# Start addresses of the operand areas in a one-core FNet and SwiGLU kernel, and w_down operands half a block later

## The chip, the cores and the metric

The kernel runs on one NeuronCore of a Trainium2 chip. The metric is device time in microseconds of one execution, inputs and outputs in HBM. TensorE (PE, with its weight loads PEld), VectorE (DVE), ScalarE (ACT), GpSimd (POOL) and SyncE (SP, which here only issues DMAs) run their own instruction streams in order and wait for each other by semaphores.

## The reference, cut to what matters

```python
# x [2048, 640]; w_gate, w_up [640, 1536]; w_down [1536, 640]
xn = layernorm(x)
a, b = xn @ dft_hid_re.T, xn @ dft_hid_im.T
s = dft_seq_re @ a - dft_seq_im @ b
g = silu((silu(xn @ w_gate) * (xn @ w_up)) @ w_down)
out = x + s * g
```

All of it is float32.

## The kernel before

Every float32 operand of a product is split into two float32r parts: the high part is written by ScalarE (line 196, a copy with rounding), the low part, what rounding lost, by VectorE (line 201, or 203 where a scale goes in). A product is then three matmuls (`mm3`, lines 217 to 219): high by high, high by low, low by high. In `nc.tensor.matmul(o, w, m)` `w` is the stationary operand, 128 columns wide, loaded into the array ahead of the matmul (PEld, LDWEIGHTS), and `m` the moving one, 512 columns of four bytes.

The work goes through stages, which one after the other keep TensorE fed: four rounds of the DFT along the sequence (`seq`, one level of Strassen's algorithm each), then twice (j = 0 and 1, half the rows each) the DFT along the hidden axis (`hid`), the gate and up products (`gate_up`) and the product with w_down (`down`). `gate_up` runs over twelve blocks f of 128 columns of w_gate and w_up. A block has the seven Strassen products p1, p5, p6, p2, p3, p7, p4, of 6, 6, 6, 9, 9, 9 and 9 matmuls: 54 for a block, 648 for twelve. Each product goes to one PSUM bank. The last one, p4, is carried into the next block, behind that block's p5.

Memory is laid out by hand. Two big tiles are areas for buffers: `hl` for split operands and `raw` for float32 data and results. A third piece of memory is handed over once: until the end of the DFT rounds it is `raw2` (float32 sums), from then on `hl2`. `gate_weights` splits the weights of a block into four buffers: the one with the operands of p1 and p5 lies in `hl`, the three others in `hl2`, so that 42 of a block's 54 matmuls load stationary operands from `hl2`. Everything else that TensorE reads in the main stages, all moving operands among it, lies in `hl`. The profile writes `ps<-hl,hl` where the stationary operand is from `hl2`, `ps<-hl` where both are from `hl`, and the order of instructions writes `hl` with a number (`hl_2545`, `hl_2549`) for `hl2`, and `raw` with a number for `raw2`.

In the built program `hl` begins at byte 16,512 of a partition (16 x 1024 + 128), `raw` at 102,528, and `raw2`/`hl2` at 200,672 (195 x 1024 + 992, which is 32 past a multiple of 64). Buffers in the operand areas have sizes that are multiples of 512 bytes, so that their places within the area are too.

The order of instructions is planned. Each step is given a planned time: products one after the other (`step`, a fixed time for each matmul), what produces operands some lead ahead (`prod`), evictions behind (`post`). The steps are then sorted by that time, and each engine and each DMA queue gets its instructions in that order. `place` and `fit` choose an offset in its area for each buffer, so that two buffers that live at once don't overlap; they prefer a pause between the last use of the one and the first write of the next, and take a smaller or a negative one where room is short. With a negative one a write waits for the earlier buffer's reader.

`down_operands` makes the stationary operands of `down` once, while the gate blocks of j = 0 run: twenty pieces (`Tp`), each with up to one VectorE sum, a split (ScalarE, then VectorE) and two stores to DRAM from POOL (line 535), from where `down` fetches them. `gate_up` takes one piece in the middle of a block and one at its end: `next(spare, None)`.

Of the kernel before, what the change touches and what calls it, by code (L numbers as in the profile page):

```python
# [7 lines left out]
F32 = mybir.dt.float32  # L8
BF16 = mybir.dt.bfloat16
F32R = mybir.dt.float32r  # L10
# [3 lines left out]
P = 128  # L14
S, D, F = 2048, 640, 1536
TC = 512
# [4 lines left out]
CG = 4  # L21
EPS = 1e-5
MM = 0.226
HL_KB, RAW_KB, TURN_KB = 84, 94, 28


class Plan:
# [111 lines left out]
def tile_fnet_swiglu(  # L139
# [17 lines left out]
    one = ctx.enter_context(tc.tile_pool(name="one", bufs=1))  # L157
    dram = ctx.enter_context(tc.tile_pool(name="dram", bufs=1, space=bass.MemoryType.DRAM))
    psum = ctx.enter_context(tc.tile_pool(name="psum", bufs=1, space=bass.MemoryType.PSUM))
    ctx.enter_context(tc.manual_schedule())  # L160

    pl = Plan()
    hl_arena = one.tile([P, HL_KB * 256], F32R, name="hl")
    raw_arena = one.tile([P, RAW_KB * 256], F32, name="raw")
    space = {"hl": hl_arena, "raw": raw_arena}
    ps = psum.tile([P, 8, TC], F32, name="ps")
    mv = one.tile([P, NS, 2], F32, name="mv")
    sm = one.tile([P, 6, NS], F32, name="sm")
    bst = one.tile([P, 2, 2, 6], F32, name="bst")
    z = one.tile([P, TC], BF16, name="z")  # L170
    rowst = one.tile([P, 2, 2 * NS], F32, name="rowst")
    mr_dram = dram.tile([2 * S], F32, name="mr_dram")
    where = {}

    def raw(name, a=0, n=None):
        o = where[name]
        arena, size = pl.size[name]
        return space[arena][:, o + a:o + (size if n is None else a + n)]

    def hl(name, i, a=0, n=None):  # L180

        key = name, "hl"[i]
        o = where[key]
        arena, size = pl.size[key]
        return space[arena][:, o + a:o + (size if n is None else a + n)]


    def split(lead, dst, n, src, reads, a=0, scale=None, sub=0, low_lead=None):


        def like(ap):
            s = src()
            return ap.rearrange("p (a b) -> p a b", b=s.shape[2]) if len(s.shape) == 3 else ap

        def high():
            nc.scalar.activation(like(hl(dst, 0, a, n)), src(), AF.Copy, scale=1.0 if scale is None else scale)  # L196

        def low():
            hi, lo = like(hl(dst, 0, a, n)).bitcast(F32), like(hl(dst, 1, a, n))
            if scale is None:  # L200
                nc.vector.tensor_tensor(lo, src(), hi, op=ALU.subtract)  # L201
            else:
                nc.vector.scalar_tensor_tensor(lo, src(), scale, hi, op0=ALU.mult, op1=ALU.subtract)  # L203

        pl.prod(lead, high, reads, [(dst, "h", sub)])
        pl.prod(lead - 2 if low_lead is None else low_lead, low, [*reads, (dst, "h", sub)], [(dst, "l", sub)])

    def both(dst, *subs):
        return [(dst, p, s) for s in (subs or (0,)) for p in "hl"]
# [27 lines left out]
    def wide(ap):  # L237
        return ap.rearrange("p (a b) -> p a b", b=TC)
# [4 lines left out]
    def evict(dst, b, a=0, n=None, after=0.0):  # L243
        n = len(b) * TC if n is None else n
        pl.post(lambda: nc.scalar.activation(wide(raw(dst, a, n)), pair(b), AF.Copy),  # L245
                pkeys(b), [(dst, a)], after)
# [163 lines left out]
    def load_x(k, lead, eng):  # L410
        pl.prod(lead, lambda: eng.dma_start(raw(xn, k * D, D), x[k * P:(k + 1) * P, :]), [], [(xn, k)])
# [144 lines left out]
    def seq(k):  # L556
        j, ri = k // 2, k % 2
# [4 lines left out]
        fresh, shared = k == 0, k == 1  # L562
# [6 lines left out]
        def source(q, g):  # L569
            c, h = j + 2 * (q // 10 - 1), q % 10 - 1  # L570
            return cs[c, ri, 2 * h + g // 2, :, 2 * (g % 2):2 * (g % 2) + 2]

        def load(q, g, lead):
            seq.n += 1
            name = pl.buf(("c", seq.n), "raw", 2 * TC)
            pl.prod(lead, lambda: nc.sync.dma_start(wide(raw(name)), source(q, g)), [], [(name, 0), (name, 1)])
            return name

# [8 lines left out]
        def operand(p, g, name):  # L587
            s = pl.buf(("S", k, p, g), "hl", 4 * TC)
            high, low = LEAD.get((p, g), LEAD.get(p, LEAD["S"])) if fresh else LEAD["S"]
            split(high, s, 2 * TC, lambda: raw(name), [(name, 0), (name, 1)], low_lead=low)  # L590
            return s
# [152 lines left out]
        def p2(g):  # L744
            if fresh:
                for kk in (8 + 2 * g, 9 + 2 * g):
                    load_x(kk, 40 + 2 * g, nc.sync)
                layer_norm(8 + 2 * g, 2, *LEAD["xn", 4 + g], nc.gpsimd)
            return operand("p2", g, load(12, g, 11 if fresh else 20))

        def p6(g):
            if shared:
# [175 lines left out]
    def gate_up(j):  # L928
        X = xn_t(j)
        for half in range(2):  # L930
            for c in (1, 2):
                pl.buf(("h", j, half, c), "raw", 6 * TC)
        tail = []
        for f in range(NF):
            w = gate_weights(j, f)
            b2, b1, b3 = (7, 5, 6) if f % 2 == 0 else (2, 3, 4)
            wkeys = [both(w[0], 0, 256), both(w[1], 0, 384), both(w[2], 0, 384), both(w[3])]

            def wt(p, i, a=0, w=w):
                part, at = COL[p]  # L940
                return hl(w[part], i, at + a, P)

            first = {}

            def go(p, bank, direct=None, wt=wt, wkeys=wkeys, first=first):
                def is_first():
                    v = first.setdefault(bank, True)
                    first[bank] = False
                    return v

                todo = []
                for k in range(2):
                    todo.append((bank, lambda i, k=k: wt(p, i, k * P),
                                 lambda i, k=k: hl(X[p], i, k * TC, TC), is_first()))
                reads = wkeys[COL[p][0]] + both(X[p])
                if direct:
                    col, half = direct
                    todo.append((bank, lambda i: wt(col, i), lambda i: hl(X[half], i), False))
                    reads += both(X[half]) + wkeys[COL[col][0]]
                product(todo, reads)  # L960

            tmp = lambda what, f=f: pl.buf((what, j, f), "raw", TC)
            hname = lambda c, f=f: ("h", j, f // 6, c)
            at = f % 6 * TC
            go("p1", b2)
            s1 = tmp("s1")
            evict(s1, (b2,))
            go("p5", b3)
            n5 = tmp("n5")
            evict(n5, (b3,))  # L970
            if tail:
                tail.pop()()
            go("p6", b2)
            u2 = tmp("u2")
            evict(u2, (b2,))
            go("p2", b1, ("d1", "d1"))
            g1 = tmp("g1")
            combine(g1, (b1,), s1, ALU.add)
            pl.post(lambda g1=g1: nc.scalar.activation(raw(g1), raw(g1), AF.Silu, scale=-1.0), [(g1, 0)], [(g1, 0)])
            if j == 0:  # L980
                next(spare, None)
            u1, u = tmp("u1"), tmp("uu")

            def top_half():
                go("p3", b3, ("d2", "d1"))
                combine(u1, (b3,), u2, ALU.subtract)
                pl.post(lambda u1=u1, g1=g1, o=hname(1), at=at: nc.vector.tensor_tensor(
                    raw(o, at, TC), raw(g1), raw(u1), op=ALU.mult), [(g1, 0), (u1, 0)], [(hname(1), at)])

            def bottom_half():  # L990
                go("p7", b2, ("d2", "d2"))
                combine(u, (b2,), n5, ALU.subtract)

            for part in (top_half, bottom_half) if f < NF - 1 else (bottom_half, top_half):
                part()

            def last(go=go, b2=b2, u=u, o=hname(2), at=at, tmp=tmp):
                go("p4", b2, ("d4", "d2"))
                g2 = tmp("g2")
                pl.post(lambda: nc.scalar.activation(raw(g2), ps[:, b2, :], AF.Silu), [("ps", b2)], [(g2, 0)])  # L1000
                pl.post(lambda: nc.vector.tensor_tensor(raw(o, at, TC), raw(g2), raw(u), op=ALU.mult),  # L1001
                        [(g2, 0), (u, 0)], [(o, at)])

            tail.append(last)
            if j == 0:
                next(spare, None)
        tail.pop()()
# [66 lines left out]
    for j in range(2):  # L1074
        hid(j)
        gate_up(j)
        down(j)

    where.update(pl.place({"hl": HL_KB * 256, "raw": RAW_KB * 256, "raw2": TURN_KB * 256, "hl2": TURN_KB * 256}))
    uses = [{pl.size[n if n in pl.size else (n, "h")][0] for n in names if n in pl.size or (n, "h") in pl.size} | {  # L1080
        pl.size[n][0] for n in names if n in pl.size} for _, _, _, names, _ in pl.ops]
    turn = 1 + max(i for i, u in enumerate(uses) if "raw2" in u)
# [58 lines left out]
```

## Time and profile before

| | |
|---|---|
| time, median of 3 runs | 994.96 us (994.18 to 995.2) |
| time of the profiled execution | 993.83 us |
| its span (first to last instruction) | 991.9 us |
| PE busy, matmuls | 984.0 us (99%), 4300 |
| DVE / ACT / POOL busy | 71% / 49% / 11% of the span |
| granted TensorE clock | 1.00 |
| DMA | 184.54 MB, 186 GB/s on average |

The profiled execution's time is 1.9 us more than its span, and 1.13 us under the median of the three runs. A busy PE is not a PE at its peak, since matmuls overlap in the records: what counts is how far apart the starts of two matmuls are.

### The profile page before, as it was taken

Reading aid. Unit: us, or ns where it says so; the run is one execution under the profiler, and the core shown is the slowest. Engines: PE = TensorE matmul, PEld = TensorE weight load, DVE = VectorE, ACT = ScalarE, POOL = GpSimd, SP = SyncE. Lnnn points to the kernel's source line nnn. Section 1 sums busy time; section 2 is a strip of 40 time slices with the busy share of each in tenths; the row PEclk is TensorE's granted clock in tenths of the full one; section 3 lists DMA queues with packets and bytes.
Section 4 is the critical chain, followed back from the end, with each engine's and each line's share of the span. In section 5 each row is a group of like instructions: output and inputs, shape, how many; then the busy total and the mean of one; then the engine's idle time right before and its main releaser. Section 6 shows DMA issues by size and latency. Waiting matters only on the chain.

```text
span 991.9 us, 11749 instructions
## 1 busy us (share of the span) xinstructions
PE 984.0 (99%) x4300; PEld 803.7 (81%) x4300; DVE 699.8 (71%) x936; ACT 483.3 (49%) x706; POOL 105.9 (11%) x173
## 2 busy tenths in 40 slices
PE   9999999999999999999999999999999999999998
PEld 5888888888888888888788888888888888888886
DVE  6899769656865685566678786587586666665675
ACT  5786456444645463334655555343345444444342
POOL 0450220011001100010211110000010000000000
PEclk9999999999999999999999999999999999999999
DMA  9995887574758477752447246679950211124675
GB/s 339 286 218 165 251 241 232 179 193 123 205 162 222 128 221 225 235 187 81 171 163 268 101 171 203 204 230 372 323 191 23 85 54 54 53 90 155 212 247 183
DMA packets 73977, 184.54 MB, mean 186 GB/s; under 512 B 6720, under 2 KB 23360, under 8 KB 73920
## 3 DMA queue, kind: packets, MB, share of 16 engines
q1 hardware_dynamic: 59808, 131.35, 39.9%
q0 software_dynamic: 14112, 52.45, 19.0%
q8 instruction: 33, 0.54, 0.2%
q14 instruction: 24, 0.20, 0.1%
HBM read 149.42 MB, written 34.36 MB: 185 GB/s over the span
## 4 chain that ended last, share of the span: by engine, by line
PE 98%; ACT 1%; issue 1%; DVE 0%; POOL 0%; POOLq 0%
PE ps L217 32%; PE ps L218 32%; PE ps L219 32%; PE ps L228 1%; PE ps L460 1%; ACT raw L245 0%; ACT hl L196 0%; ACT L1088 0%; DVE raw L250 0%; POOL y_dram L839 0%; DVE hl L203 0%; DVE hl L201 0%; DVE raw L1059 0%; DVE raw L1061 0%; DVE raw L914 0%
## 5 line engine op out<-in xcount | busy, mean ns | idle before, releaser
L196 ACT ACTIVATE hl<-raw 128x1024 fp32r<-128x1024 f32 (+7 forms) x499 | 360.4, 765 | 284.7 <-PE ps L219 74.8
L201 DVE TENSOR_TENSOR hl<-raw,hl 128x1024 fp32r<-128x1024 f32 (+5 forms) x428 | 375.7, 907 | 136.3 <-ACT hl L196 72.1
L217 PE MATMUL ps<-hl 128*128 128x512 f32 x1088 | 422.8, 389 | 0.0
L218 PE MATMUL ps<-hl 128*128 128x512 f32 x1088 | 422.5, 388 | 0.0
L219 PE MATMUL ps<-hl 128*128 128x512 f32 x1088 | 422.0, 388 | 0.0
L217 PEld LDWEIGHTS ps<-hl 128*128 128x128 f32 x1088 | 204.3, 188 | 43.0 <-ACT hl L196 0.4
L218 PEld LDWEIGHTS ps<-hl 128*128 128x128 f32 x1088 | 204.3, 188 | 42.6 <-DVE hl L201 0.3
L219 PEld LDWEIGHTS ps<-hl 128*128 128x128 f32 x1088 | 204.3, 188 | 42.3 <-DVE hl L203 0.2
L245 ACT ACTIVATE raw<-ps 128x512 f32<-128x512 f32 (+1 forms) x120 | 78.3, 670 | 119.9 <-PE ps L219 117.4
L217 PE MATMUL ps<-hl,hl 128*128 128x512 f32 x336 | 133.3, 397 | 1.1 <-ACT raw L245 1.1
L218 PE MATMUL ps<-hl,hl 128*128 128x512 f32 x336 | 133.1, 396 | 0.0
L219 PE MATMUL ps<-hl,hl 128*128 128x512 f32 x336 | 133.1, 396 | 0.0
L250 DVE TENSOR_TENSOR raw<-ps,raw 128x512 f32<-128x512 f32 (+1 forms) x93 | 74.7, 804 | 62.9 <-PE ps L219 61.6
L217 PEld LDWEIGHTS ps<-hl,hl 128*128 128x128 f32 x336 | 63.3, 188 | 16.9 <-ACT raw L245 1.5
L219 PEld LDWEIGHTS ps<-hl,hl 128*128 128x128 f32 x336 | 63.3, 188 | 15.5
L218 PEld LDWEIGHTS ps<-hl,hl 128*128 128x128 f32 x336 | 63.2, 188 | 15.2
L1001 DVE TENSOR_TENSOR raw<-raw 128x512 f32<-128x512 f32 x24 | 16.6, 692 | 50.9 <-ACT raw L1000 50.9
L203 DVE SCALAR_TENSOR_TENSOR hl<-raw,hl 128x384 fp32r<-128x384 f32 (+4 forms) x71 | 41.2, 580 | 10.2 <-ACT hl L196 4.6
L914 DVE TENSOR_TENSOR raw<-raw 128x256 f32<-128x256 f32 (+1 forms) x96 | 47.8, 519 | 0.0
L581 POOL DMA_DIRECT2D raw<-in_cs x36 | 32.1, 964 | 124.2 <-DVE raw L584 65.4
L1063 POOL DMA_DIRECT2D out<-raw x10 | 6.7, 673 | 306.9 <-DVE raw L1061 215.7
L658 POOL DMA_DIRECT2D p_dram<-raw x24 | 17.4, 766 | 204.3 <-DVE raw L250 164.9
(55 smaller groups left out, 305.9 us busy)
## 6 DMA issues: line engine op xcount, KB each, us to landing
raw<-in_cs SPq DMA_DIRECT2D x82, 512.0 KB, 6.9
hl<-d_p SPq DMA_DIRECT2D x56, 384.0 KB, 4.0
raw<-in_cs POOLq DMA_DIRECT2D x36, 512.0 KB, 9.5
raw<-in_wb SPq DMA_DIRECT2D x24, 640.0 KB, 3.9
d_p<-hl POOLq DMA_DIRECT2D x28, 384.0 KB, 3.4
raw<-p_dram SPq DMA_DIRECT2D x8, 1280.0 KB, 9.8
p_dram<-raw POOLq DMA_DIRECT2D x16, 512.0 KB, 6.3
raw<-in_hd SPq DMA_DIRECT2D x20, 320.0 KB, 9.2
```

The lines of the kernel that those rows point to most:

```text
L196: nc.scalar.activation(like(hl(dst, 0, a, n)), src(), AF.Copy, scale=1.0 if scale is None else scale)
L201: nc.vector.tensor_tensor(lo, src(), hi, op=ALU.subtract)
L203: nc.vector.scalar_tensor_tensor(lo, src(), scale, hi, op0=ALU.mult, op1=ALU.subtract)
L217: nc.tensor.matmul(o, w(0), m(0), start=first, stop=False, skip_group_check=True)
L218: nc.tensor.matmul(o, w(0), m(1), start=False, stop=False, skip_group_check=True)
L219: nc.tensor.matmul(o, w(1), m(0), start=False, stop=True, skip_group_check=True)
L245: pl.post(lambda: nc.scalar.activation(wide(raw(dst, a, n)), pair(b), AF.Copy), pkeys(b), [(dst, a)], after)
L250: pl.post(lambda: nc.vector.tensor_tensor(wide(raw(dst, a, n)), pair(b), wide(raw(other)), op=op), [*pkeys(b), (other, 0)], [(dst, a)], after)
L581: pl.prod(lead, lambda: nc.gpsimd.dma_start(wide(raw(name)), source(q, g), accum_op=ALU.add), [], [(name, 0), (name, 1)], 8)
L658: pl.post(lambda: nc.gpsimd.dma_start(p_dram[ri, c, e0:e0 + len(b)].rearrange("k p t -> p k t"), wide(raw(name))), [(name, 0)], [("pd", ri ...
L914: pl.prod(lead, lambda o=o, a=a, b=b, op=op: nc.vector.tensor_tensor(o(), a(), b(), op=op), [(w, 0)], [(c, lead)])
L1001: pl.post(lambda: nc.vector.tensor_tensor(raw(o, at, TC), raw(g2), raw(u), op=ALU.mult), [(g2, 0), (u, 0)], [(o, at)])
```

## The change

The big tiles are allocated in another order. The small tiles come first, with a filler of 32 bytes, then `hl`; `raw` goes to a pool at the other end of the memory; the piece that is handed over (`raw2`, later `hl2`) then begins right behind `hl`. In the built program `hl` begins at 18,432 (18 x 1024), `raw2`/`hl2` at 103,424 (101 x 1024) and `raw` at 132,096. `hl` is 1 KB smaller (83 KB) and `raw` 992 bytes larger, so that all offsets are placed anew. Two of the loads of the first DFT round (p2, g = 1 and 2) go to `raw2` in place of `raw`. The first of the calls for w_down operands in `gate_up` is left out, so that each of the twenty pieces is made half a block later.

```diff
-HL_KB, RAW_KB, TURN_KB = 84, 94, 28
+HL_KB, RAW_KB, TURN_KB = 83, 95, 28
...
-    hl_arena = one.tile([P, HL_KB * 256], F32R, name="hl")
-    raw_arena = one.tile([P, RAW_KB * 256], F32, name="raw")
-    space = {"hl": hl_arena, "raw": raw_arena}
-    ps = psum.tile([P, 8, TC], F32, name="ps")
     mv = one.tile([P, NS, 2], F32, name="mv")
...
     rowst = one.tile([P, 2, 2 * NS], F32, name="rowst")
+    one.tile([P, 8], F32, name="pad")
+    right = ctx.enter_context(tc.tile_pool(name="right", bufs=1, side="right"))
+    space = {"hl": one.tile([P, HL_KB * 256], F32R, name="hl"), "raw": right.tile([P, RAW_KB * 256 - 8], F32, name="raw")}
+    ps = psum.tile([P, 8, TC], F32, name="ps")
...
-        def load(q, g, lead):
+        def load(q, g, lead, arena="raw"):
             seq.n += 1
-            name = pl.buf(("c", seq.n), "raw", 2 * TC)
+            name = pl.buf(("c", seq.n), arena, 2 * TC)
...
-            return operand("p2", g, load(12, g, 11 if fresh else 20))
+            return operand("p2", g, load(12, g, 11 if fresh else 20, "raw2" if fresh and g in (1, 2) else "raw"))
...
-            if j == 0:
+            if j == 0 and f:
                 next(spare, None)
...
-    where.update(pl.place({"hl": HL_KB * 256, "raw": RAW_KB * 256, "raw2": TURN_KB * 256, "hl2": TURN_KB * 256}))
+    where.update(pl.place({"hl": HL_KB * 256, "raw": RAW_KB * 256 - 8, "raw2": TURN_KB * 256, "hl2": TURN_KB * 256}))
```

On ScalarE, at the end of the first gate block of j = 0, this stood before (768 columns: a piece of w_down; `hl_2545`: gate weights; `raw<-ps`: evictions):

```order
L979 ACTIVATE raw<-raw 128x512 [waits DVE_49]
L196 ACTIVATE hl<-raw 128x768 [waits DMAHW4_49]
L196 ACTIVATE hl_2545<-raw 128x384
L196 ACTIVATE hl<-raw 128x768 [waits DMAHW5_49,DMASW3_49,DVE_49]
L196 ACTIVATE hl_2545<-raw 128x256 [waits DVE_49]
L245 ACTIVATE raw<-ps 128x512 [waits DMASW0_49,PE_49]
```

Now the first piece stands at the block's end, where the second one was, and waits for its weights alone:

```order
L979 ACTIVATE raw<-raw 128x512 [waits DVE_49]
L196 ACTIVATE hl_2549<-raw 128x384
L196 ACTIVATE hl<-raw 128x768 [waits DMAHW4_49]
L196 ACTIVATE hl_2549<-raw 128x256 [waits DVE_49]
L245 ACTIVATE raw<-ps 128x512 [waits DMASW0_49,PE_49]
```

The second piece follows in the middle of the next block, and waits for no store any more (DMASW: a semaphore of POOL's DMAs):

```order
L196 ACTIVATE hl_2549<-raw 128x256 [waits DVE_49,Activation_49]
L196 ACTIVATE hl_2549<-raw 128x384
L979 ACTIVATE raw<-raw 128x512 [waits DMASW6_49,DVE_49]
L196 ACTIVATE hl<-raw 128x768 [waits DMAHW5_49]
L196 ACTIVATE hl_2549<-raw 128x384
```

On VectorE, where the hidden DFT ends and the gate blocks of j = 0 begin, this stood before (the 1024-wide row is the low part of the moving operand of p7; `hl_2545` are the low parts of the first gate weights):

```order
L914 TENSOR_TENSOR raw<-raw 128x256
L201 TENSOR_TENSOR hl<-raw,hl 128x512 [waits Activation_49]
L201 TENSOR_TENSOR hl<-raw,hl 128x1024 [waits Activation_49]
L201 TENSOR_TENSOR hl_2545<-raw,hl_2545 128x256 [waits Activation_49]
L203 SCALAR_TENSOR_TENSOR hl_2545<-raw,hl_2545 128x384 [waits Activation_49]
```

Now the order is the same, but the 1024-wide row's new place is one that the last step of the hidden DFT reads, and it waits for TensorE too:

```order
L914 TENSOR_TENSOR raw<-raw 128x256
L201 TENSOR_TENSOR hl<-raw,hl 128x512 [waits Activation_49]
L201 TENSOR_TENSOR hl<-raw,hl 128x1024 [waits PE_49,Activation_49]
L201 TENSOR_TENSOR hl_2549<-raw,hl_2549 128x256 [waits Activation_49]
L203 SCALAR_TENSOR_TENSOR hl_2549<-raw,hl_2549 128x384 [waits Activation_49]
```

On SP, in the first DFT round, the order of the loads is the same, and two of them have another target:

```order
 L576 DMA raw<-in_cs 128x1024 x4
 L411 DMA raw<-in_x 128x640 x8
-L576 DMA raw<-in_cs 128x1024 x72
+L576 DMA raw<-in_cs 128x1024
+L576 DMA raw_107<-in_cs 128x1024 x2
+L576 DMA raw<-in_cs 128x1024 x69
```

The DMAs that belong to a piece of w_down (its two stores on POOL, and its fetches by `down` on SP) keep their order among themselves; only the stores stand half a block later.

## The prediction, made before the changed kernel was run

> **What bounds the kernel now.** First the page: the busy times, the chain that ended last, and the groups of matmuls.
>
> ```profile
> span 991.9 us, 11749 instructions
> PE 984.0 (99%) x4300; PEld 803.7 (81%) x4300; DVE 699.8 (71%) x936; ACT 483.3 (49%) x706; POOL 105.9 (11%) x173
> PE 98%; ACT 1%; issue 1%; DVE 0%; POOL 0%; POOLq 0%
> L217 PE MATMUL ps<-hl 128*128 128x512 f32 x1088 | 422.8, 389 | 0.0
> L217 PE MATMUL ps<-hl,hl 128*128 128x512 f32 x336 | 133.3, 397 | 1.1 <-ACT raw L245 1.1
> ```
>
> TensorE sets the end: 98% of the chain is its own, and it waits for almost nothing. So only two things can move the time: the distance between matmuls, and the few gaps. The two groups (each is one of three lines, so 3,264 and 1,008 matmuls) already differ: with the stationary operand in `hl2` a record lasts 397 ns, else 389. Records overlap, so I measure the distance of starts. Next, therefore, the table by stretches: the gate and up products of j = 0 and of j = 1 as first and third row, and between them 100 us of other products (`down` and `hid`), from `hl` alone; under it the starts at the edges.
>
> ```profile
> 468.55:620.95 152.40, 151.30 (x650) 121.68 (x649) 116.79 (x217) 83.99 (x166) 24.35 (x45) 1.00 0.52 177
> 650.00:750.00 100.00, 100.00 (x443) 82.84 (x442) 71.22 (x71) 41.48 (x55) 6.74 (x11) 1.00 0.79 266
> 762.42:913.48 151.06, 151.06 (x650) 121.90 (x648) 95.64 (x189) 70.95 (x145) 2.70 (x5) 1.00 0.23 75
> ...
> 468.55 0.39 PE L217 MATMUL ps<-hl 128*128 128x512 f32 x1
> 620.95 0.40 PE L217 MATMUL ps<-hl 128*128 128x512 f32 x1
> 649.77 0.39 PE L218 MATMUL ps<-hl 128*128 128x512 f32 x1
> 749.96 0.39 PE L219 MATMUL ps<-hl 128*128 128x512 f32 x1
> 762.42 0.39 PE L217 MATMUL ps<-hl 128*128 128x512 f32 x1
> 913.48 0.40 PE L217 MATMUL ps<-hl 128*128 128x512 f32 x1
> ```
>
> The columns after the length are PE, PEld, DVE, ACT and POOL with their counts, then the granted clock. In the middle row 443 matmuls start from 649.77 to 749.96, so 100.19/442 = 226.67 ns apart. Twelve gate blocks have 648 matmuls (the counts of 650 take in one at each edge): 152.40/648 = 235.2 ns and 151.06/648 = 233.1 ns. The clock is 1.00 in all three, so it isn't the clock. Then one block, from the timeline:
>
> ```profile
> 520.89 0.39 PE L217 MATMUL ps<-hl,hl 128*128 128x512 f32 x1
> 525.80 0.39 PE L217 MATMUL ps<-hl,hl 128*128 128x512 f32 x1
> ...
> 532.57 0.39 PE L219 MATMUL ps<-hl 128*128 128x512 f32 x1
> 533.25 0.39 PE L219 MATMUL ps<-hl 128*128 128x512 f32 x1
> ```
>
> With weights from `hl2`, 21 steps take 4.91 us, 233.8 ns each; at the end of p5, with weights from `hl` and the same kind of moving operand, bank and neighbours, three steps take 0.68 us, 226.7 ns. The slow pace goes with the area of the stationary operand. `hl2` begins 32 bytes past a multiple of 64 and `hl` at a multiple of 128, which is the difference that the change takes away.
>
> The other loss is one gap, 483.61 to 485.11. ScalarE's timeline, POOL's, the DMA issues around 479.6 (count, KB, us to landing) and TensorE's tell its cause.
>
> ```profile
> 477.49 1.24 ACT L196 ACTIVATE hl<-raw 128x768 fp32r<-128x768 f32 x2
> 479.61 0.54 POOL L535 DMA_DIRECT2D d_p<-hl  x1 [0.45 <-DVE hl L203]
> d_p<-hl POOLq DMA_DIRECT2D x1, 384.0 KB, 3.7
> 483.42 1.15 ACT L196 ACTIVATE hl<-raw 128x768 fp32r<-128x768 f32 x2 [4.69 <-issue]
> 484.48 0.58 ACT L245 ACTIVATE raw<-ps 128x512 f32<-128x512 f32 x1
> ...
> 483.61 0.40 PE L219 MATMUL ps<-hl,hl 128*128 128x512 f32 x1
> 485.11 0.50 PE L217 MATMUL ps<-hl,hl 128*128 128x512 f32 x1 [1.10 <-ACT raw L245]
> 485.45 0.40 PE L218 MATMUL ps<-hl,hl 128*128 128x512 f32 x1
> ...
> 532.14 1.15 ACT L196 ACTIVATE hl<-raw 128x768 fp32r<-128x768 f32 x2 [2.86 <-issue]
> ```
>
> The second w_down piece stood idle for 4.69 us. The first piece's store was issued at 479.61 and landed 3.7 us later, at 483.3; at 483.42 ScalarE went on: the second piece had been placed where the first one still waited to be stored. Behind it in ScalarE's queue stood the eviction (484.48) that frees the bank of the next product. The gap costs 1.50 + 0.34 - 2 x 0.234 = 1.37 us. A like wait of 2.86 us at 532.14 cost TensorE nothing.
>
> **The change part by part.** Alignment: 648 matmuls at 226.67 ns take 146.88 us. The two gate stages stand above it by 5.52 and 4.18 us, 9.70 together, of which the gap is 1.37. The pace is thus worth 4.15 + 4.18 = 8.33 us, if an `hl2` at a multiple of 1024 bytes runs as `hl` does. Its bounds: 0, if the start isn't the cause; and more than 8.33, if the start of `hl` (128 past a multiple of 1024) costs something too, which no row excludes. I take 8.33, because the hl rows, in the same block, are the nearest.
>
> [...]
>
> The pieces half a block later: in the new order the first piece is alone at the end of block 0 and the second, in the middle of block 1, waits for no store. The gap goes, 1.37 us. What is late next: every later piece moves by half a block, with its VectorE sum, its two stores on POOL, which has 24.35 us of work in 152.40 and nothing else queued there, and the weights behind the pieces on ScalarE, 84 of 152 us busy. The last store lands half a block, about 6 us, nearer to its fetch on SP, but its product is the last of `down`. Cost 0; if the cover is gone, another wait like that of 532.14, free, or like that of 483.42, 1.37 us.
>
> New offsets: 1 KB less in `hl` and all buffers placed anew can put new waits anywhere, and take old ones away. The two rows with 4.69 and 2.86 us bound one: 1.37 us or 0. One can be read from the new order: VectorE's 1024-wide low part of p7's operand now waits for the last step of the hidden DFT.
>
> ```profile
> L201 DVE TENSOR_TENSOR hl<-raw,hl 128x1024 fp32r<-128x1024 f32 x170 | 203.2, 1221 | 77.9 <-ACT hl L196 43.5 <-PE ps L219 14.9 <-issue 13.8
> ...
> 468.32 0.39 PE L219 MATMUL ps<-hl 128*128 128x512 f32 x1
> 471.27 0.39 PE L217 MATMUL ps<-hl,hl 128*128 128x512 f32 x1
> ...
> 466.26 2.16 DVE L201 TENSOR_TENSOR hl<-raw,hl 128x512 fp32r<-128x512 f32 x3
> 474.98 0.69 DVE L250 TENSOR_TENSOR raw<-ps,raw 128x512 f32<-128x512 f32 x1 [2.84 <-PE ps L219]
> ```
>
> That step's last matmul ends at 468.71. The row then takes 1.22 us, and the low part of p6's weights behind it 0.42: 470.35, and p6 begins at 471.27. Everything behind is some 1.9 us later than before (the three rows from 466.26 were done at 468.42; now 470.35) and runs into 2.84 us in which VectorE stood idle. Cost 0; without that cover 1.9. With shorter blocks VectorE would be busy for 116.79 of 147 us, 79%: no bound. I take 0 for all placement, 0 to 2 x 1.37 for the range. The two loads that go to `raw2` keep their place in SP's queue: 0.
>
> Sum against the profiled execution: 993.83 - 8.33 - 1.37 = 984.1. That execution stood 1.13 us under the median of the runs, so for a median 994.96 - 9.70 = **985.3 us**.
>
> **The rivals.** *The start isn't the cause* (the slow pace belongs to something else of those 42 matmuls). For it: the trace has `hl2` at one place only, and no second misaligned area of this type. Against it: p5's rows above. Only the gap goes: 994.96 - 1.37 = 993.6, which is 0.14% and counts as no change (0.2%, 2 us, is about what a measurement of this kernel can tell from none). [...]
>
> *The other matmuls get slower.* All 3,264 whose operands are both in `hl` move too, from 128 past a multiple of 1024 to a multiple, and both operands then begin on the same boundary. If that brought them to 233.8 ns: 3,264 x 7.1 ns = 23.2 us; with the gate still slow, 994.96 + 23.2 - 1.4 = 1016.8. It decides from 9.70/7.1 ns = 1,370 slowed matmuls on, if the gate is cured. For it: no row shows such a start. Against it: weights and moving operands in `hl` share their boundary today too, and run faster than the pair that doesn't.
>
> *All get faster.* What a matmul costs beyond its columns can be read from the last ones, of 256 columns:
>
> ```profile
> 985.29 0.28 PE L219 MATMUL ps<-hl 128*128 128x256 f32 x1
> 987.09 0.28 PE L219 MATMUL ps<-hl 128*128 128x256 f32 x1
> ```
>
> Fifteen steps, 120.0 ns each; a column is (226.67 - 120.0)/256 = 0.417 ns, 512 are 213.3, and 13.3 ns are fixed (20.5 in `hl2`). If the 128 bytes cause all of them, 4,272 x 13.3 ns = 57 us go, to 928. Against it: 13.3 ns would have to hang on a start that is a multiple of 128 already. [...]
>
> *As forecast, with one or two new waits of 1.37 us*: 986.7 to 988.0.
>
> **How the numbers follow.** Forecast as summed 0.74; with new waits 0.10; start not the cause 0.08; others slower 0.03; all faster 0.05. The time is the likeliest's, 985.3. The range: down to 983.5, since the profiled execution's sum is 984.1 and new offsets may take small waits away; up to 989.0, two new waits (988.0) and 1.0 for the spread of the runs. It leaves out the last three cases, 0.16. Faster by over 0.2%: 0.74 + 0.10 + 0.05 = 0.89, less 0.01 for a cure by parts; within: 0.08; slower: 0.03, and 0.01 for several waits in places that I didn't see.
>
> **What would show it.** Right: starts 226.7 ns apart through whole gate blocks, records of `ps<-hl,hl` at 389 ns as the others, 146.9 us from first gate matmul to first of `down`, no wait of over 1 us before a 768-wide split near 483 us, PE gaps nowhere but in the first 20 us. Wrong: a pace of 233.8 in the gate blocks (start not the cause), another pace than 226.67 in 650 to 750 us (the last two rivals), or a new gap with VectorE named at the start of a gate stage.

## The result and the profile after

The changed kernel takes 985.79 us (median of 4 runs, 985.51 to 986.28), the kernel before 995.08 us: ratio 0.9909, 95% interval 0.9892 to 0.9926. The forecast was 985.3 us. The profiled executions differ by less, 985.85 against 993.83 us, since that of before lies 1.25 us under its median. The page of the kernel after, busy times, chain and the two groups of matmuls:

```profile
span 984.1 us, 11734 instructions
PE 976.2 (99%) x4300; PEld 803.5 (82%) x4300; DVE 700.2 (71%) x936; ACT 483.8 (49%) x706; POOL 106.5 (11%) x173
PE 99%; DVE 0%; ACT 0%; issue 0%; DVEq 0%
L217 PE MATMUL ps<-hl 128*128 128x512 f32 x1088 | 422.4, 388 | 0.0
L217 PE MATMUL ps<-hl,hl 128*128 128x512 f32 x336 | 131.1, 390 | 1.0 <-ACT raw L245 1.0
```

The records with weights from `hl2` have come down from 397 to 390 ns, to those from `hl`. The stretches, in the order of those of before (first matmul of the gate blocks to the first of `down`, for j = 0, then 650 to 750 us, then j = 1):

```profile
468.81:617.39 148.58, 147.53 (x650) 121.38 (x648) 118.38 (x220) 84.02 (x166) 24.35 (x45) 1.00 0.56 199
650.00:750.00 100.00, 100.00 (x443) 82.78 (x442) 71.15 (x72) 40.12 (x55) 5.45 (x9) 1.00 0.77 257
758.83:905.71 146.88, 146.88 (x650) 121.62 (x648) 94.26 (x186) 71.09 (x145) 2.70 (x5) 1.00 0.23 75
```

The stage of j = 1 takes 146.88 us for 648 matmuls, 226.67 ns each: as forecast, 4.18 us less. The stage of j = 0 stands 1.70 us above that. The old gap near 483 us is gone, and a new one has come at the stage's start. Timelines of VectorE, ScalarE and TensorE there:

```profile
469.08 1.56 DVE L201 TENSOR_TENSOR hl<-raw,hl 128x1024 fp32r<-128x1024 f32 x2 [4.87 <-PE ps L219]
470.55 0.55 DVE L203 SCALAR_TENSOR_TENSOR hl<-raw,hl 128x384 fp32r<-128x384 f32 x1
471.02 1.16 DVE L914 TENSOR_TENSOR raw<-raw 128x256 f32<-128x256 f32 x2
...
471.48 0.72 ACT L196 ACTIVATE hl<-raw 128x256 fp32r<-128x256 f32 x2 [3.67 <-DVE raw L914]
472.11 0.58 ACT L245 ACTIVATE raw<-ps 128x512 f32<-128x512 f32 x1
...
471.30 0.39 PE L219 MATMUL ps<-hl 128*128 128x512 f32 x1
472.74 0.50 PE L217 MATMUL ps<-hl,hl 128*128 128x512 f32 x1 [1.05 <-ACT raw L245]
```

VectorE waits for the end of the hidden DFT (4.87 us idle), as the new order of waits said. Its weight sum (line 914) ends late, and ScalarE's split of that sum waits 3.67 us for it: it begins 2.67 us after the first gate matmul, where before it began 0.70 us after it (469.25 and 468.55). Behind that split in ScalarE's queue stands the eviction (472.11) of p1, whose bank p6 needs. TensorE starts p6 at 472.74 in place of 471.53. The next matmul follows after 0.34 us, so that the gap costs 1.32 us.

Two smaller gaps, at 532 and 593 us, have VectorE's combination late behind a w_down sum; one of them, from the weight loads:

```profile
532.06 0.19 PEld L217 LDWEIGHTS ps<-hl,hl 128*128 128x128 f32 x1 [0.30 <-DVE raw L250]
```

### The profile page after: what moved, and what is told of

Its sections match the earlier page's. It is cut to its first block, busy times and chain, and to the rows that moved or that the text cites. A ratio compares the mean times of both kernels' runs of the same rounds, so it can differ in the third digit from the quotient of the medians.

```text
span 984.1 us, 11734 instructions
## 1 busy us (share of the span) xinstructions
PE 976.2 (99%) x4300; PEld 803.5 (82%) x4300; DVE 700.2 (71%) x936; ACT 483.8 (49%) x706; POOL 106.5 (11%) x173
## 4 chain that ended last, share of the span: by engine, by line
PE 99%; DVE 0%; ACT 0%; issue 0%; DVEq 0%
PE ps L217 33%; PE ps L219 33%; PE ps L218 33%; PE ps L460 1%; PE ps L228 1%; DVE hl L201 0%; ACT L1088 0%; ACT raw L245 0%; DVE hl L203 0%; DVE raw L1059 0%; DVE raw L1061 0%; ACT hl L196 0%; ACT raw L1055 0%; DVE raw L914 0%; ACT z L1088 0%
## 5 line engine op out<-in xcount | busy, mean ns | idle before, releaser
L217 PE MATMUL ps<-hl,hl 128*128 128x512 f32 x336 | 131.1, 390 | 1.0 <-ACT raw L245 1.0
L219 PE MATMUL ps<-hl,hl 128*128 128x512 f32 x336 | 130.7, 389 | 0.0
L218 PE MATMUL ps<-hl,hl 128*128 128x512 f32 x336 | 130.7, 389 | 0.0
```

The source lines that it names most:

```text
L217: nc.tensor.matmul(o, w(0), m(0), start=first, stop=False, skip_group_check=True)
L218: nc.tensor.matmul(o, w(0), m(1), start=False, stop=False, skip_group_check=True)
L219: nc.tensor.matmul(o, w(1), m(0), start=False, stop=True, skip_group_check=True)
```

## The experiments

Times are medians, with the kernel before run beside them on the same chip: 994.26 us for the first four experiments, 994.06 us (one run) for the next four, 994.24 us for the last four. The cleanest measure of the pace is the stage of j = 1, which has no gap in most kernels: 146.88 us when all its matmuls are 226.67 ns apart, 151.06 us in the kernel before.

### hl2 alone at a multiple of 1024

```diff
-                [P, TURN_KB * 256], F32R, name="hl2")
+                [P, TURN_KB * 256], F32R, name="hl2")[:, 8:]
```

> The kernel before, with one edit: hl2 begins 32 bytes later, at byte 200,704 (196 x 1024), still at the top of the memory. Order, offsets and everything else as before. Theory 1 (the start of the stationary operand sets the pace): 226.7 ns a matmul in all gate blocks, 8.3 us less, and the gap of 1.4 us near 483 us stays: about 986.8 us. Theory 2 (the high location of hl2, or the gate stage itself, sets it): pace stays at 234 ns, no change, 995.1 us.

992.21 us, ratio 0.9978 (0.9968 to 0.9987). The stretch of j = 1:

```profile
761.36:911.19 149.83, 149.83 (x649) 1.00 0.23 75
```

Both theories miss. 149.83 us is 231.2 ns a matmul: `hl2` at a multiple of 1024 gets 1.23 of the 4.18 us. The start of the stationary operand alone is not what the pace hangs on, and the place high in the memory isn't all of it either, or nothing would have moved. (Here, and wherever the start of `hl2` is moved below, `place` is given 256 bytes less for that area, and buffers inside it move by multiples of 512 bytes.)

### The pieces half a block later, alone, and with that shift

```diff
-            if j == 0:
+            if j == 0 and f:
                 next(spare, None)
```

> The kernel before with the w_down pieces half a block later and nothing else (offsets are placed anew by the planner). Theory 1 (the gap comes from the second piece placed over the first one's pending store): no gap near 483 us, pace still 234 ns in the gate blocks, about 993.7 us. Rival (a new wait takes its place, as in the changed kernel): 995 us or a gap of over 1 us elsewhere.

> The kernel before with both: hl2 32 bytes later and the pieces half a block later; the big tiles stay where they were. Theory 1 (the two effects add, and the new gap at 471 us of the changed kernel comes from its new offsets): no gap, 226.7 ns, 995.1 - 8.3 - 1.4 = 985.4 us. Rival (the changed kernel's gap at 471 us comes from the faster pace or the later pieces): a gap of 1.3 us at 471 us, 986.7 us.

998.5 us, ratio 1.0038 (1.0023 to 1.0053), and 995.83 us, ratio 1.0011 (1.0001 to 1.002): the first slower than before, the second no gain. The gap near 483 us is gone in both. But offsets in `hl` were placed anew in both, and TensorE waits at the start of the gate stage, longer than in the changed kernel and behind the same last links: ScalarE waits for VectorE's weight sum, and the eviction stands behind its split. In the first of the two, VectorE ahead of j = 0, then TensorE at the start of j = 0 and of j = 1:

```profile
458.87 0.69 DVE L201 TENSOR_TENSOR hl<-raw,hl 128x512 fp32r<-128x512 f32 x1 [6.75 <-PE ps L219]
...
471.17 0.39 PE L219 MATMUL ps<-hl 128*128 128x512 f32 x1
473.79 0.50 PE L217 MATMUL ps<-hl,hl 128*128 128x512 f32 x1 [2.23 <-ACT raw L245]
...
766.18 0.39 PE L219 MATMUL ps<-hl 128*128 128x512 f32 x1
767.61 0.50 PE L217 MATMUL ps<-hl,hl 128*128 128x512 f32 x1 [1.05 <-ACT raw L245]
```

2.62 and 1.43 us from start to start, where 0.23 is due: 3.6 us, more than the 1.37 us that left. At j = 0 VectorE doesn't wait there as it does in the changed kernel: it works almost without a pause, but some 3 us behind the kernel before, after an earlier wait of 6.75 us for TensorE in the hidden DFT. By these gaps the first kernel would take 994.26 - 1.37 + 3.6 = 996.5 us. Its profiled execution took 996.97 us, at a granted clock of 0.999; the three others, at 0.997 and 0.998, took 998.4 to 998.8 us. Of the second kernel's ten executions six, at 0.998, took 995.7 to 996.5 us and four, at 1.000, 994.1 to 995.0 us. So both medians seem to hold a term of the clock too, of some 1.5 us (the last section has the profiles).

The piece that was moved does what was said of it, and the placement that follows decides what it is worth. The gaps that the two rivals named came, but the second's were larger than named, and so was its time (995.83 us, not 986.7). The gap doesn't need the faster pace: in the first kernel the pace is that of before.

### p7's split behind the hidden DFT

```diff
-        keep("p7", a[11], 5)
+        keep("p7", a[11], 1)
```

> The changed kernel with the split of p7's moving operand planned 4 matmul-times-of-the-planner (us) later, behind the hidden DFT's last step. Theory 1 (the gap of 1.32 us at 471 us comes from VectorE waiting there for TensorE, ScalarE waiting for VectorE's weight sum, and the eviction behind it): the gap goes, 985.8 - 1.3 = 984.5 us. Rival (ScalarE is late by its own work, or the eviction waits for something else): the gap stays, 985.8 us.

984.46 us (984.17 to 985.04), ratio 0.9899 (0.9883 to 0.9916). The median is 1.33 us under the changed kernel's, but the kernel before, run beside each of the two, differs by 0.8 us as well (994.26 and 995.08), so that the nearness to the gap of 1.32 us says little. The profiled executions are 0.81 us apart (985.04 and 985.85): the stage of j = 0 is 1.50 us shorter and begins 0.64 us later. The stage of j = 0, and TensorE at its start:

```profile
469.45:616.53 147.08, 147.08 (x650) 1.00 0.50 184
...
471.94 0.39 PE L219 MATMUL ps<-hl 128*128 128x512 f32 x1
472.17 0.39 PE L217 MATMUL ps<-hl,hl 128*128 128x512 f32 x1
...
471.00 0.60 ACT L245 ACTIVATE raw<-ps 128x512 f32<-128x512 f32 x1 [2.67 <-PE ps L219]
```

p6 starts on time, the eviction now waits for TensorE, and the stage is down to 147.08 us. The chain is shown: VectorE's wait, ScalarE's wait for VectorE, the eviction behind. This version has the lowest median of all.

### hl2 16, 32 and 64 bytes on, hl 32 bytes on

The changed kernel, with the slice of `hl2` beginning at element 4, 8 or 16, or that of `hl` at element 8:

```diff
-                [P, TURN_KB * 256], F32R, name="hl2")
+                [P, TURN_KB * 256], F32R, name="hl2")[:, 4:]
```

> The changed kernel with hl2 beginning 16 bytes later (a multiple of 16, not of 32). Theory A (a stationary operand has to begin at a multiple of 64): about 234 ns in the gate blocks, 994 us. Theory B (a multiple of 16 is enough, or 32): 226.7 ns, 985.8 us.

> The changed kernel with hl2 beginning 32 bytes later, so 32 past a multiple of 64 as before, but low in the memory and right behind hl. Theory A (start at a multiple of 64): 234 ns, 994 us. Rival (the high location was the cause): 226.7 ns, 985.8 us.

> The changed kernel with hl2 beginning 64 bytes later: a multiple of 64, not of 128. Theory A (multiple of 64 is enough): 226.7 ns, 985.8 us. Rival (it has to be 128 or more): about 234 ns, 994 us.

> The changed kernel with hl, not hl2, beginning 32 bytes later: all moving operands, and the stationary ones of all stages but the gate's 42 of 54 matmuls, are 32 past a multiple of 64. Theory A (only the stationary operand's start counts): gate matmuls from hl2 at 226.7 ns with misaligned moving operands, all others at 234 ns: about 985.8 + 3,264 x 7.1 ns = 1009 us. Rival (the moving operand counts too, or alone): gate matmuls from hl2 over 226.7 ns, and the others at more than 234 ns if both add.

986.44, 991.99, 992.81 and 994.65 us, one run each. The stretches of j = 1, in this order, and for the last kernel also 650 to 750 us:

```profile
759.42:906.30 146.88, 146.88 (x649) 1.00 0.23 75
...
761.46:911.80 150.34, 150.34 (x650) 1.00 0.23 74
...
762.14:912.66 150.52, 150.52 (x649) 1.00 0.22 74
...
763.48:914.13 150.65, 150.65 (x649) 1.00 0.20 67
650.00:750.00 100.00, 100.00 (x443) 1.00 0.81 268
```

With 16 bytes the pace stays, with 32 or 64 it is lost: theory A fails at both ends, since 16 is no multiple of 64 and 64 is one. The last kernel is the key. Its gate matmuls from `hl2` have weights at a multiple of 512 and moving operands 32 bytes past one, and are slow. Its other stages have both operands 32 bytes past one, and run 443 matmuls in the same 100 us as before and after. What counts in these kernels is how the two operands lie to each other. (This kernel also has a gap of 1.29 us of its own at 548 us, behind a w_down split that stood idle for 5.65 us; its `hl` was placed anew, with less room.)

### Both areas alike, but on no round address

From this came a new theory, R: the pace is the full one when stationary and moving operand begin at the same place modulo 512 bytes, or less. In the kernel before, `hl2` is moved by 160 bytes, so that it begins 128 past a multiple of 512, as `hl` does:

```diff
-                [P, TURN_KB * 256], F32R, name="hl2")
+                [P, TURN_KB * 256], F32R, name="hl2")[:, 40:]
```

> The kernel before, with one edit: hl2 begins 160 bytes later, at byte 200,832, which is 128 past a multiple of 512, as hl is; no area is at a multiple of 512. Order and offsets as before. New theory R (the pace depends on where the stationary operand lies relative to the moving one, modulo 512 bytes or less, not on either start alone): 226.7 ns in all gate blocks, 8.3 us less, gap near 483 us as before: about 986 us. Old theory A (starts at a multiple of 512 or 1024 are needed): 232 to 234 ns, 993 to 995 us.

In the fastest version, a filler of 64 in place of 32 bytes moves everything from `hl` on (`raw` gives up 32 bytes):

```diff
-    one.tile([P, 8], F32, name="pad")
+    one.tile([P, 16], F32, name="pad")
```

> The changed kernel with p7's split later, as in the run on that, and with everything from hl on 32 bytes later: hl, hl2 and raw all begin 32 past a multiple of 512; same order, same waits. Theory R (only the relation of the two operands counts): 226.7 ns throughout, 984.5 us, as without the shift. Theory A (absolute starts count): about 234 ns in all matmuls, 984.5 + 4,272 x 7.1 ns = 1015 us.

986.74 us (986.41 to 987.37), ratio 0.9925 (0.9913 to 0.9938), and 984.64 us (984.17 to 985.65), ratio 0.9905 (0.989 to 0.992). The stretches of the first (j = 1, j = 0), then of the second (j = 1, and 650 to 750 us):

```profile
759.48:906.36 146.88, 146.88 (x649) 1.00 0.24 77
468.69:618.04 149.35, 148.15 (x649) 1.00 0.53 180
...
757.69:904.57 146.88, 146.88 (x649) 1.00 0.21 71
650.00:750.00 100.00, 100.00 (x443) 1.00 0.79 261
```

Theory R holds in both, and absolute starts count for nothing here. One number in the kernel before gives 7.5 of the 9.3 us, with the order, the offsets in `hl` and the old gap as they were.

The stage of j = 0 in the first kernel is 1.10 us longer than 146.88 us and the old gap of 1.37 us. Three weight loads, at 482, 532 and 594 us, now wait for a combination on VectorE, which cost 0.27, 0.31 and 0.34 us; the last of them:

```profile
594.11 0.19 PEld L217 LDWEIGHTS ps<-hl,hl 128*128 128x128 f32 x1 [0.49 <-DVE raw L250]
```

The kernel before doesn't lose this time: its stage of j = 0, 152.40 us, is that of j = 1, 151.06 us, and the old gap of 1.37 us, to 0.03 us. So here the faster pace itself uncovered small waits, with no buffer in `hl` moved.

### Many distances in one kernel

The weights in `hl2` were moved by another distance in each gate block:

```diff
+        if arena == "hl2":
+            o += SHIFT[name[1]][name[2]] // 4
```

> The changed kernel with the gate weights in hl2 moved by another number of bytes in each gate block: 0, 4, 8, 12, 16, 20, 24, 28, 32, 48, 64, 80 in the blocks of j = 0, and 96 to 184 in steps of 8 in those of j = 1 (hl stays at a multiple of 1024, hl2's offsets are placed with 96 bytes between buffers). Theory R with lines of 32 bytes: 226.7 ns below 32 bytes, 232 to 234 ns from 32 on. R with lines of 64: blocks at 32 are fast as well, which the earlier run at 32 excludes. If the pace fell steadily with the distance instead, blocks at 4 to 28 would stand between.

> As the last, with 192, 208, 224, 232, 240, 248, 256, 264, 272, 280, 284, 288 bytes in the blocks of j = 0 and 432, 448, 464, 480, 488, 496, 500, 504, 508, 512, 520, 528 in those of j = 1. Theory R with a period of 512 bytes: slow everywhere but from 512 on (and perhaps from 485 to 511). With a period of 256: fast around 256 to 287 too.

990.63 and 990.79 us, one run each; the stage of j = 1 in the two:

```profile
760.80:910.50 149.70, 149.70 (x649) 1.00 0.22 74
...
760.91:910.63 149.72, 149.72 (x650) 1.00 0.22 74
```

These two don't answer their question. The 96 bytes left between buffers made high and low parts of one block start at different places modulo 512, so each block mixed several distances, and nearly all ran between 230 and 234 ns (the stage of j = 1 at 231.0 ns on average in both). They tell nothing of the width of the good range (16 bytes are in it, 32 not) or of a period under 512.

But they show a limit of R. From the first of them, the starts at the two ends of a row of 9 matmuls and of a row of 18 (lines 223 to 225 are here what 217 to 219 are elsewhere):

```profile
473.83 0.39 PE L223 MATMUL ps<-hl,hl 128*128 128x512 f32 x1
475.93 0.40 PE L223 MATMUL ps<-hl,hl 128*128 128x512 f32 x1
...
804.44 0.39 PE L223 MATMUL ps<-hl,hl 128*128 128x512 f32 x1
808.52 0.39 PE L223 MATMUL ps<-hl 128*128 128x512 f32 x1
```

By the offsets that `place` gives, six of the nine have weights that begin where their moving operand does, modulo 512, and three, the low parts, weights 96 bytes past it. They take 2.10 us, 233 ns each. The 18 have weights 376 and 472 bytes past, and take 4.08 us, 226.7 ns each. In both kernels together, 27 matmuls with equal starts were measured: the next one started 232.0 ns later on average, and 231.8 ns after the others from `hl2`. So R isn't a rule for one matmul and its own two operands. It holds in the kernels above, where all gate weights in `hl2`, high and low parts, lie at one distance. What holds where they don't is open.

## Why the prediction was right, and where it wasn't

- **The pace, 8.33 us**: right in size. j = 1 gave 4.18 of 4.18; j = 0, without its gaps, about 4.1 of 4.15.
- **Its cause**: wrong. The step "`hl2` begins 32 bytes past a multiple of 64 and `hl` at a multiple of 128, which is the difference that the change takes away" failed. Moving `hl2` to a multiple of 1024 in the kernel before brought 1.23 us in j = 1, moving it to the same place as `hl` modulo 512 brought all of it. The change worked because it put both areas on the same boundary. That the size came out right is luck in so far: `hl` moved to a multiple of 1024 as well, and the sum counted that for nothing. The prediction had the better sentence in a rival, that weights and moving operands in `hl` share their boundary and run faster than the pair that doesn't, and didn't draw the conclusion.
- **The old gap, 1.37 us**: gone, as said; the second piece's split waits for no store any more, and it stays away in both kernels that only make the pieces later or move `hl2` besides.
- **New offsets, taken at 0**: this term was mis-sized. The wait of p7's low part was named, and its 1.9 us on VectorE too, but only VectorE's own cover and p6's weights were followed. ScalarE, which waits for VectorE's weight sum, and the eviction behind it weren't. It cost 1.32 us. The range held it: one new wait, 986.7.
- **VectorE at 79% with shorter blocks, "no bound"**: this step failed by a little. The two small gaps at 532 and 593 us cost about 0.15 us each, and the kernel with the old offsets and the faster pace has three of up to 0.34. The busy share is an average over the stage; behind work for a w_down piece, a combination on VectorE came late.
- **The others get slower, all get faster**: neither; 443 matmuls in 650 to 750 us, before and after. The 13.3 ns that the prediction worked out as fixed (an estimate, from 226.67 ns for 512 columns and 120.0 for 256) don't hang on the start, as far as it was moved (0, 32 and 128 past a multiple of 512).

The sum of the profiled executions: the gate stages 3.82 and 4.18 us shorter, their start 0.26 us later (468.81 against 468.55), which is 7.74 of the 7.8 us between the spans. The forecast sum was 9.70; what is missing is the new gaps (1.70) and that start. (In the profiles of all the kernels here the stage begins between 468.35 and 469.45 us.) The median came out as near as 0.5 us to the forecast by luck: the runs of before, 995.08 us, lie 1.25 us above their profiled execution and those of after 0.06 under theirs, and what the former have more isn't in a trace.

## What to carry to other kernels

Where the distance of matmuls differs between stages at the same clock (here 233.1 and 226.67 ns), compare the start addresses of the two operands with each other, before any absolute alignment, and move a whole area, so that all its operands keep one distance. Here the faster stage uncovered small waits (0.15 to 0.34 us each) that a busy share of 79% for VectorE didn't show. A new placement of buffers is an edit of its own (here it cost 1.32 us): look for writes that now wait for a late reader, and follow not only the engine that waits but the engines that wait for it, down to the eviction that frees a PSUM bank. Half an edit can be slower than none: here the later pieces alone cost 0.4%.

## What the runs showed of the hardware that wasn't expected

- Where all stationary operands of the gate stage began at the same place modulo 512 bytes as the moving ones, matmuls ran at 226.67 ns, at 0, 32 and 128 past a multiple of 512; with 16 bytes between the two also. With `hl2` 32 bytes past or short of `hl`'s place, 64 past, 128 short or 352 past, the stage of j = 1, where it has no gap, averaged 231.2 to 233.1 ns. Where high and low parts lay at different distances, equal starts of one matmul's operands did not bring the full pace, and some unlike ones had it. Why, and where between 16 and 32 bytes the edge lies, stays open.
- After the gap of 2.62 us at the start of the gate stage, the granted clock was 0.56 on average over 3.9 us in one profile (the pieces later and `hl2` moved), with 12 matmuls in place of 18, and stayed at 1.00 in the other (the pieces later alone), with the same gap. The stretch 474.3 to 478.2 us in the one and the other:

```profile
474.30:478.20 3.90, 3.90 (x12) 0.56 0.27 101
...
474.30:478.20 3.90, 3.90 (x18) 1.00 0.32 120
```
